# Chunk 0 of an RWKV scan read two tokens a partition, with rstd on ScalarE and a new instruction order

## The chip, the core and the metric

The kernel runs on one core of a Trainium2 chip. A core has five engines, each with its own instruction queue: TensorE (PE, matmuls), VectorE (DVE), ScalarE (ACT), GpSimd (POOL) and SyncE (SP, which here only issues DMAs). Sixteen DMA engines move the data. The metric is the device time of one execution in microseconds, as the median over runs; lower is better.

## What is computed

Two layers in one launch: a linear-attention scan over 768 tokens (4 batches, 8 heads, head size 48), then a LayerNorm and a two-matrix MLP (384 to 1536 to 384) with a residual.

```python
for t in range(S):
    kt, vt, rt = k[:, :, t], v[:, :, t], r[:, :, t]
    cur = np.einsum('bhd,bhe->bhde', u[None] * kt, vt)
    y[:, :, t] = np.einsum('bhd,bhde->bhe', rt, state + cur)
    state = w[None, :, :, None] * state + np.einsum('bhd,bhe->bhde', kt, vt)

x = y.transpose(0, 2, 1, 3).reshape(B, S, H * D)
xn = (x - mean(x)) / np.sqrt(var(x) + 1e-06) * g_ln
out = x + np.maximum(xn @ w_ch1, 0.0) @ w_ch2
```

## The kernel before

The scan is cut into 6 chunks of 128 tokens for each of 4 batches: 24 pieces, numbered `i = 4 * chunk + batch`. Within a piece the decay is folded into the operands: r is multiplied by w^t and k by w^(-1-t), so that the sum over earlier tokens becomes a masked product of two 128-token matrices, and the state `Z` carries what lies before the chunk. Pieces 0 to 3 (chunk 0) have no state behind them.

One piece passes through these steps, whose two- or three-letter names are functions of the kernel and stand in the order table:

- `LR`, `LK`, `LV` (lines 329, 326, 332) issue the loads of r, k, v from SP. A token lies on a partition, and each of its 8 heads is 48 numbers, 192 bytes, at another place in memory.
- `SR`, `SK` scale r and k by the tables `Fr` and `Fk` into the bf16 tile `sc`; `CV` casts v into `vv`. All three go through helpers at lines 194 and 191.
- `TR` (line 348) transposes both on PE; `TCr`, `TCk` or `TC` copy the result from PSUM to `trs`. `Q` (194) multiplies r and k for the `u` term.
- `AT` (371) makes the 8 products of 128 by 128, `AM`, `AMa`, `AMb` (381) mask them into `A`.
- `S` (402, 409, 415) makes the `u` term and the new state, `CC`, `ZU`, `ZD` take them out of PSUM, and `VB` (434) scales v by the `u` term.
- `Y` (444, 452) makes the output, `X` (459) adds `VB` and sums the row, `SQ` (466) squares, `XN` (472, 474) centres.
- `LT` (512) and `XT` transpose the centred rows on PE, or `LT2`, `LTD` do so by DMA.

The MLP follows in 17 groups of one or two pieces (`GROUPS`): `UP` (527) is the first product, `RL` (543, 545) the ReLU, `RS` (480, 483) makes 1/std on POOL in two instructions, `DN` (557) is the second product, `OT` (615) adds the residual and `STO` (622) stores. `LW1` loads a third of `w_ch1` (line 301), and `SW` (308, 310, 312) scales a third of a third into bf16; `LW2` (318) and `CW` do the same for `w_ch2`, into the same fp32 tiles.

The first part of the launch makes the tables: `WF`, `LC` load w, u and the gain; `WB` (269) spreads w over the partitions on PE; `TL` loads the activation table; `LN`, `FK`, `FR` make the logarithm, `Fk` and `Fr` on ACT; `CT`, `CP` turn w, u and the gain into columns; `DU` (261, 265) are matmuls of zeros whose result nobody reads.

Nothing is scheduled by the compiler: `PLAN` is a text of steps `name,piece,engine`, and each engine runs its own instructions in the order in which the text names them. `SLOTS` gives the number of buffers of each ring.

```python
    for step in PLAN.split():
        name, i, e = step.split(",")
        steps[name](int(i), e)
```

## Time and profile before

| | |
|---|---|
| median of 3 runs | 149.1 us (147.78 to 149.59) |
| profiled execution, its own time | 148.24 us |
| its span, first to last instruction | 146.5 us |
| PE, DVE, POOL, ACT busy | 93%, 75%, 64%, 55% of the span |
| mean granted TensorE clock | 0.965 |
| packets moved by DMA | 99267, of which 94508 under 512 B |

Busy shares are means over stages that differ, so the stage has to be looked at by itself. A row of the windows gives, for a stretch of time, each engine's busy microseconds with its number of instructions in brackets, then the granted TensorE clock as a share of full speed, the mean busy share of the 16 DMA engines, and the GB/s that they moved. In the timelines a row is start, duration, engine, line, operation, `out<-in`, shapes and a count of merged instructions; in square brackets stands idle time before it and what ended it. In the chain of waits a row is start, duration, engine, tile and line of the work that ended last at that time. Instructions of one engine overlap at their ends, so two that follow each other take less than the sum of their durations.

### The profile page before, as it was taken

How to read it: one execution, taken by the hardware profiler on the slowest of the kernel's cores; microseconds unless marked ns; L12 is line 12 of the kernel's file. 1: busy time of each engine (PE TensorE's matmuls, PEld its weight loads, DVE VectorE, ACT ScalarE, POOL GpSimd, SP SyncE). 2: the span in 40 equal slices, each digit the busy share in tenths (PEclk: the TensorE clock that was granted, in tenths of full speed). 3: DMA queues.
4: the chain of work that ended last, by engine and by line, in shares of the span. 5: the costliest groups of instructions: out<-in, count | busy, mean ns of one | idle time of the engine just before them, and what ended most of it. 6: DMA issues, size and time to landing. Idle time of an engine off the chain costs nothing.

```text
span 146.5 us, 4250 instructions
## 1 busy us (share of the span) xinstructions
PE 135.8 (93%) x1693; PEld 108.2 (74%) x1693; DVE 110.5 (75%) x220; ACT 80.1 (55%) x175; POOL 94.0 (64%) x132
## 2 busy tenths in 40 slices
PE   3966699999999999999999999999999999999991
PEld 1455477998687897787688887966877777888871
DVE  4569999767969899985959948897946796875232
ACT  2575577977676467466386560663654752244600
POOL 4089878967888999989957493428553076644030
PEclk9999556999999999999999999999999999999999
DMA  5999899999889999899999999988999997830114
GB/s 97 209 211 221 175 277 401 194 258 380 231 170 188 206 197 232 156 215 242 96 229 206 260 233 186 217 166 185 245 157 199 229 184 156 206 123 0 54 37 182
DMA packets 99267, 28.59 MB, mean 195 GB/s; under 512 B 94508, under 2 KB 97712, under 8 KB 99248
## 3 DMA queue, kind: packets, MB, share of 16 engines
q1 hardware_dynamic: 98352, 27.24, 86.3%
q10 hardware_dynamic: 896, 1.09, 2.0%
q8 instruction: 13, 0.21, 0.6%
q14 instruction: 6, 0.05, 0.1%
HBM read 18.88 MB, written 4.72 MB: 161 GB/s over the span
## 4 chain that ended last, share of the span: by engine, by line
PE 60%; SPq 11%; DMA 11%; DVE 7%; POOL 6%; issue 4%; DVEq 0%; POOLq 0%
PE hp L527 17%; PE o L557 16%; PE s L557 7%; PE s L527 5%; SPq L332 4%; DMA w_f<-in_moe_w_ch_dram 4%; SPq L329 4%; SPq L326 3%; DMA trs<-sc 3%; DMA rf<-in_r_dram 3%; PE o L527 3%; PE at L371 2%; PE hp L452 2%; POOL sc L194 2%; PE at L348 2%
## 5 line engine op out<-in xcount | busy, mean ns | idle before, releaser
L527 PEld LDWEIGHTS <-w_sb 128*128 128x128 bf16 x612 | 47.9, 114 | 2.4 <-POOL w_sb L312 0.4
L527 PE MATMUL hp<-xT,w_sb 128*128 128x128 bf16 (+1 forms) x408 | 39.9, 244 | 0.3 <-POOL w_sb L312 0.3
L557 PEld LDWEIGHTS <-hT 128*128 128x128 bf16 x276 | 25.2, 97 | 13.7 <-issue 0.4
L557 PE MATMUL o<-w_sb,hT 128*128 128x384 bf16 x180 | 34.5, 326 | 0.0
L543 ACT ACTIVATE hT<-hp 128x512 bf16<-128x512 f32 x41 | 24.3, 597 | 18.2 <-PE hp L527 17.7
L381 DVE TENSOR_TENSOR A<-at,mask 128x1024 bf16<-128x1024 f32 (+1 forms) x27 | 28.9, 1096 | 1.2 <-PE at L371 1.2
L194 POOL TENSOR_TENSOR sc<-kf,Fk 128x384 bf16<-128x384 f32 x14 | 14.5, 1044 | 10.5 <-DMA kf<-in_k_dram 10.4
L434 POOL TENSOR_TENSOR Vb<-vf,cc 128x384 f32<-128x384 f32 x17 | 14.7, 868 | 8.7 <-ACT cc L189 3.6
L557 PE MATMUL s<-w_sb,hT 128*128 128x384 bf16 x96 | 18.9, 326 | 0.2 <-DVE x L459 0.2
L194 POOL TENSOR_TENSOR q<-trs 128x512 bf16<-128x512 bf16 x11 | 13.4, 1220 | 5.5 <-PE hp L527 2.6
L194 POOL TENSOR_TENSOR sc<-rf,Fr 128x384 bf16<-128x384 f32 x12 | 13.0, 1082 | 5.3 <-DMA rf<-in_r_dram 5.3
L466 ACT ACTIVATE sqj<-x,sm 128x384 bf16<-128x384 f32 x24 | 14.7, 611 | 1.4 <-DVE x L459 1.3
L615 DVE SCALAR_TENSOR_TENSOR ot<-o,rs,x 128x384 f32<-128x384 f32 x15 | 9.2, 613 | 4.5 <-POOL rs L483 2.8
L459 DVE SCALAR_TENSOR_TENSOR x<-hp,Vb 128x384 f32<-128x384 f32 x19 | 10.5, 554 | 2.3 <-PE hp L452 1.6
L483 POOL TENSOR_TENSOR rs<-rs,expo 128x1 f32<-128x1 f32 (+1 forms) x17 | 10.6, 625 | 1.4
L472 ACT ACTIVATE xn<-x,sm 128x384 bf16<-128x384 f32 x13 | 8.0, 613 | 5.7 <-DVE x L459 5.6
L371 PE MATMUL at<-trs 48*128 48x128 bf16 x192 | 8.6, 229 | 2.4 <-ACT trs L189 1.2
L527 PE MATMUL s<-xT,w_sb 128*128 128x128 bf16 (+1 forms) x120 | 10.8, 235 | 0.0
L194 POOL TENSOR_TENSOR Z<-ZS,WLZ 128x384 bf16<-128x384 f32 x10 | 10.3, 1030 | 0.6 <-DVE ZS L428 0.6
L545 DVE TENSOR_SCALAR hT<-hp 128x512 bf16<-128x512 f32 x9 | 6.2, 689 | 4.6 <-PE hp L527 4.6
L371 PEld LDWEIGHTS <-trs 48*128 48x128 bf16 x192 | 6.0, 99 | 4.9 <-ACT trs L189 2.1
L194 DVE TENSOR_TENSOR sc<-rf,Fr 128x384 bf16<-128x384 f32 x12 | 7.5, 633 | 2.3 <-DMA rf<-in_r_dram 2.2
(116 smaller groups left out, 214.3 us busy)
## 6 DMA issues: line engine op xcount, KB each, us to landing
rf<-in_r_dram SPq DMA_DIRECT2D x24, 192.0 KB, 3.8
kf<-in_k_dram SPq DMA_DIRECT2D x24, 192.0 KB, 3.9
vf<-in_v_dram SPq DMA_DIRECT2D x24, 192.0 KB, 3.9
w_f<-in_moe_w_ch_dram SPq DMA_DIRECT2D x6, 768.0 KB, 7.2
out_dram<-ot SPq DMA_DIRECT2D x18, 192.0 KB, 3.4
out_dram<-ot ACTq DMA_DIRECT2D x5, 192.0 KB, 2.0
trs<-sc SPq DMA_TRANSPOSE x12, 3.9
xT<-xn SPq DMA_TRANSPOSE x9, 2.8
```

Of the source, the lines that this page charges most:

```text
L194: engines[e].tensor_tensor(out=out, in0=in0, in1=in1, op=ALU.mult)
L371: nc.tensor.matmul(out=t[:, par, q, :], lhsT=trs(i)[p0 : p0 + D, 1, q, :], rhs=trs(i)[p0 : p0 + D, 0, q, :], start=True, stop=True,)
L381: nc.vector.tensor_tensor(out=AA(i)[:, a:b].rearrange("p e q t -> p (e q) t"), in0=psum["at", i][:, a:b].rearrange("p e q t -> p (e q) t") ...
L434: engines[e].tensor_tensor(out=Vb(i)[:].rearrange("p (h d) -> p h d", h=H), in0=vf(i)[:], in1=cc(i)[:].unsqueeze(2).to_broadcast([P, H, D] ...
L459: nc.vector.scalar_tensor_tensor(out=xx(i)[:], in0=psum["y", i][:, :C], scalar=1.0, in1=Vb(i)[:], op0=ALU.mult, op1=ALU.add, accum_out=sm[ ...
L466: nc.scalar.activation(out=sqj[:], in_=xx(i)[:], func=ACT.Square, bias=sm[i][:], scale=-float(C), accum_out=sq[g][:, j : j + 1])
L472: nc.scalar.activation(out=xn(i), in_=xx(i)[:], func=ACT.Identity, bias=sm[i][:], scale=-float(C))
L483: nc.gpsimd.tensor_tensor(out=rs[g][:], in0=rs[g][:], in1=expo[:, :n], op=ALU.pow)
L527: nc.tensor.matmul(out=t[:, a * gw : (a + 1) * gw].rearrange("p (j t) -> p j t", j=size), lhsT=w1_sb[n][kc][:, fb::FB], rhs=xT(g)[:, :size ...
L543: nc.scalar.activation(out=o, in_=s, func=ACT.Relu)
L557: nc.tensor.matmul(out=psum["o", i][:, :C], lhsT=hT(g)[:, fk, j * P : (j + 1) * P], rhs=w2_sb[d][:, a, :], start=(seen == 0 and a == 0), s ...
L615: nc.vector.scalar_tensor_tensor(out=ot(i), in0=psum["o", i][:, :C], scalar=rs[g][:, j : j + 1], in1=xx(i)[:], op0=ALU.mult, op1=ALU.add,)
```

## The change

For pieces 0 to 3 the layout is another. A tile of `kf`, `rf` or `vf` now holds two pieces. For chunk 0, partition p (0 to 63) holds tokens 2p and 2p+1 of an even batch, and partition 64+p the same tokens of the odd batch: each packet is the 96 numbers of two neighbouring tokens, 384 bytes, and a load is 512 packets instead of 1024. What a step works on as piece `i` is then one token parity of both batches. There are four tables `F0` (k and r, even and odd tokens), made from the powers `pow0`, and masks `mask0` for parities. `AT` makes 16 products with 64 output rows instead of 8 with 128; the state part of `S` takes two pieces of 64 rows, 8 products instead of 4; `Y` of one batch gathers from both parity pieces, 32 products instead of 8. The stores of these pieces write 3072 contiguous bytes from 64 partitions.

`RS` moves to ACT, as `Ln` and `Exp` of a column. `VB` may run on ACT, as 8 instructions of 48 columns. `ln_all` and `Fr` share a tile. The rings `kf`, `rf` go from 11 to 10 buffers, `x` from 14 to 12, `A` from 3 to 4. The whole `PLAN` is in another order with other engines; two of its lines stand for it.

```diff
-SLOTS = {'kf': 11, 'rf': 11, 'vf': 11, ..., 'A': 3, ..., 'x': 14, ...}
+SLOTS = {'kf': 10, 'rf': 10, 'vf': 11, ..., 'A': 4, ..., 'x': 12, ...}
 PLAN = """
-LR,1,- LK,0,- MI,0,g MW,0,v WF,0,s WB,0,- LC,0,s LC,1,s MM,0,g MP,0,v TL,0,s LC,2,s DU,21,h LN,0,s FK,0,s FR,0,s SK,0,v LK,1,- LR,0,- SK,1,v CT,0,o
+MZ,0,g MI,0,g MM,0,g WF,0,s MW,0,v LC,0,s LC,2,s LC,1,s WB,0,h LK,1,- LV,0,- LR,1,- LR,0,- TL,0,s LN,0,s MP,0,v MQ,0,v LK,0,- GK,0,s SK,0,g CT,0,o
...
+    def GK(x, e):
+        nc.scalar.activation(out=F0[x][1][:], in_=ln_all[:], func=ACT.Exp, scale=pow0[:, x, 1:2])
+    def GR(x, e):
+        nc.scalar.activation(out=F0[x][0][:], in_=ln_all[:], func=ACT.Exp, scale=pow0[:, x, 0:1])
...
+    def load(ring, pair, src, i):
+        if i >= B:
+            nc.sync.dma_start(out=ring(i), in_=chunk_src(src, i))
+        else:
+            b0 = i % 2 * DP
+            nc.sync.dma_start(
+                out=pair[i // 2][b0 : b0 + DP].rearrange("p a h d -> p (a h d)").rearrange("p (h x) -> p h x", h=H),
+                in_=src[i, :, :L, :].rearrange("h (p j) d -> p h (j d)", j=2),
+            )
...
     def SK(i, e):
-        times(e, sck(i)[:, :, :D], kf(i)[:], Fk[:])
+        times(e, sck(i)[:, :, :D], rows_of(kf, kp, i), Fk[:] if i >= B else F0[i % 2][1][:])
...
     def AT(i, e):
         t = psum["at", i] = ps_a.tile([P, 2, HP, P], FP32, name="at")
+        if i < B:
+            for q in range(HP):
+                for b0 in (0, DP):
+                    for par in range(2):
+                        p0 = par * DP
+                        nc.tensor.matmul(
+                            out=t[b0 : b0 + DP, par, q, :].rearrange("p (j t) -> p j t", j=2),
+                            lhsT=trs(i)[p0 : p0 + D, 1, q, b0 : b0 + DP],
+                            rhs=tp[i // 2][p0 : p0 + D, :, 0, q, b0 : b0 + DP],
+                            start=True,
+                            stop=True,
+                        )
+            return
...
     def VB(i, e):
+        if e == "s":
+            for h in range(H):
+                nc.scalar.activation(out=o[:, h], in_=rows_of(vf, vp, i)[:, h], func=ACT.Copy, scale=cc(i)[:, h : h + 1])
...
     def Y(i, e):
+        if i < B:
+            x = i % 2 * DP
+            for a in (i - i % 2, i - i % 2 + 1):
+                for par in range(2):
+                    for q in range(HP):
+                        h = 2 * q + par
+                        for b0 in (0, DP):
+                            nc.tensor.matmul(
+                                out=t[b0 : b0 + DP, h * D : (h + 1) * D], lhsT=AA(a)[b0 : b0 + DP, par, q, x : x + DP],
+                                rhs=vv(a)[b0 : b0 + DP, h, :],
+                                start=first, stop=True, skip_group_check=True,
+                            )
+                        first = False
+            return
...
     def RS(g, e):
-        nc.gpsimd.tensor_scalar(
-            out=rs[g][:], in0=sq[g][:], scalar1=1.0 / C, scalar2=1e-6 * C * C, op0=ALU.mult, op1=ALU.add
-        )
-        nc.gpsimd.tensor_tensor(out=rs[g][:], in0=rs[g][:], in1=expo[:, :n], op=ALU.pow)
+        nc.scalar.activation(out=rs[g][:], in_=sq[g][:], func=ACT.Ln, bias=eps[:], scale=1.0 / C)
+        nc.scalar.activation(out=rs[g][:], in_=rs[g][:], func=ACT.Exp, scale=-0.5)
```

At three places the order counts most. The rows below give the line, the operation, the tile written (its number is that of a buffer) and the tiles read.

ACT at the start of the program, before: the table load stands ahead of the last small DMA, and two tables follow the logarithm.

```order
L204 DMA w_row<-in_w_dram 1x384
L212 DMA rows<-in_w_dram 4x2x48
L212 DMA rows<-in_u_dram 4x2x48
L230 ACT_TABLE_LOAD
L210 DMA rows<-in_moe_g_ln_dram 3x128
L272 ACTIVATE ln_all<-s 128x384
L277 ACTIVATE Fk<-ln_all,pow_i 128x384
L280 ACTIVATE Fr<-ln_all,pow_i 128x384
L189 COPY trs_112<-hp 128x512 x2
L189 COPY cols<-o 128x11
```

And ACT at the same place now, where the tile `Fr` first holds the logarithm:

```order
L220 DMA rows<-in_moe_g_ln_dram 3x128
L222 DMA rows<-in_u_dram 4x2x48
L240 ACT_TABLE_LOAD
L307 ACTIVATE Fr<-hp 128x384
L273 ACTIVATE F_01_214<-Fr,pow_217 128x384
L199 COPY cols<-o 128x11
L312 ACTIVATE Fk<-Fr,pow_i 128x384
L276 ACTIVATE F_10_215<-Fr,pow_217 128x384
L276 ACTIVATE F_00_213<-Fr,pow_217 128x384
L273 ACTIVATE F_11_216<-Fr,pow_217 128x384
L315 ACTIVATE Fr<-Fr,pow_i 128x384
L199 CAST vv_91<-vf_79 128x384
```

All four small DMAs now stand ahead of the table load, and six tables are made where two were, with the copy of the columns and a cast of v among them.

SP around the first load of `w_ch1`, before (`w_f` is its fp32 tile; 18 loads of r, k, v stand ahead of it, of which these are the last):

```order
L329 DMA rf_85<-in_r_dram 128x8x48
L332 DMA vf_94<-in_v_dram 128x8x48
L332 DMA vf_95<-in_v_dram 128x8x48
L332 DMA vf_96<-in_v_dram 128x8x48
L301 DMA w_f_243<-in_moe_w_ch_dram 128x3x512
```

And SP there now, where 17 loads stand ahead of it, 12 of them with the new 64x8x96 shape:

```order
L368 DMA vf_80<-in_v_dram 64x8x96
L365 DMA rf_76<-in_r_dram 128x8x48
L368 DMA vf_80<-in_v_dram 64x8x96
L365 DMA vf_81<-in_v_dram 128x8x48
L365 DMA rf_76<-in_r_dram 128x8x48
L365 DMA kf_71<-in_k_dram 128x8x48 x2
L336 DMA w_f_228<-in_moe_w_ch_dram 128x3x512
```

The load of v for piece 5 has moved behind the three loads of `w_ch1`; the other 17 are still ahead of them.

ACT before the first `UP` product, before (`w_sb` is the scaled part of `w_ch1`, `xT` the transposed rows, `hT` what `RL` writes):

```order
L189 COPY xT_157<-o 128x384
L189 CAST vv_110<-vf_94 128x384
L189 COPY cc_126<-o 128x8
L466 ACTIVATE sqj,sq_192<-x_141,sm_168 128x384
L189 COPY trs_112<-at 128x1024
L189 COPY xT_158<-at 128x384
L472 ACTIVATE xn_155<-x_142,sm_169 128x384
L189 COPY cc_127<-hp 128x8
L308 ACTIVATE w_sb_1_247<-w_f_243,g_neg 128x512
```

And now:

```order
L507 ACTIVATE Vb_118<-vf_79,cc_105 128x48 x8
L558 ACTIVATE xn_134<-x_123,sm_148 128x384
L199 COPY trs_97<-hp 128x1024
L199 CAST vv_94<-vf_81 128x384
L552 ACTIVATE sqj,sq_172<-x_123,sm_148 128x384
L343 ACTIVATE w_sb_1_232<-w_f_228,g_neg 128x512
L343 ACTIVATE w_sb_0_231<-w_f_228,g_neg 128x512
L199 COPY xT_137<-at 128x384
L199 COPY xT_138<-at 128x384
```

Both transposed rows are now copied after the weights are scaled, and the eight-part `VB` stands ahead of them all.

On PE, the first `UP` now comes ahead of the two products `AT` of pieces 4 and 5, of `S` of piece 5, of `Y` of piece 4 and of the `LT` of piece 2, all of which stood before it.

More of the change, by code (lines that the diff above doesn't have):

```diff
@@ L356, in TC @@
     def TC(i, e):
-        copy(e, trs(i)[:], psum["tr", i][:].rearrange("p (a q) t -> p a q t", a=2))
+        copy(e, trs(i), psum["tr", i][:].rearrange("p (a q) t -> p a q t", a=2))
     def Q(i, e):
@@ L412, in S_ @@
                 )
-            flat = sck(i).rearrange("p (q e) d -> p q (e d)", e=2)
-            for q in range(HP):
-                nc.tensor.matmul(
-                    out=t[:, q * E2 : (q + 1) * E2], lhsT=flat[:, q, :], rhs=vv(i)[:, 2 * q : 2 * q + 2, :],
-                    start=False, stop=True, skip_group_check=True,
-                )
+            if i >= B:
+                parts = [(i, slice(0, P))]
+            else:
+                b0 = i % 2 * DP
+                parts = [(i - i % 2 + x, slice(b0, b0 + DP)) for x in range(2)]
+            for a, rows_ in parts:
+                flat = sck(a).rearrange("p (q e) d -> p q (e d)", e=2)
+                for q in range(HP):
+                    nc.tensor.matmul(
+                        out=t[:, q * E2 : (q + 1) * E2], lhsT=flat[rows_, q, :], rhs=vv(a)[rows_, 2 * q : 2 * q + 2, :],
+                        start=False, stop=True, skip_group_check=True,
+                    )
     def CC(i, e):
@@ L497, in TKR @@
         nc.sync.dma_start_transpose(
[L498 removed]
+            out=trs(i).rearrange("p a q t -> p (a q) t"), in_=sc(i)[:].rearrange("p a h d -> p (a h d)")
         )
```

162 lines of the change are left out of this document (99 added, 63 removed).

## The prediction

> **What bounds the kernel now.** I read first the page's rows of slices, then the windows of the first 25 us, then the chain of waits, then the timelines of the engines in that part. From the page:
>
> ```profile
> PE   3966699999999999999999999999999999999991
> PEclk9999556999999999999999999999999999999999
> ```
>
> A slice is 3.66 us. From the seventh on, PE is full and its clock is whole. So the kernel has two parts: a start of some 25 us in which PE is not full, and 118 us in which PE's work sets the time. A change pays if PE becomes full earlier, less what work it then still has ahead.
>
> ```profile
> 5.00:10.00 5.00, 4.29 (x42) 2.79 (x41) 3.41 (x8) 2.75 (x8) 2.44 (x4) 1.00 1.08 216
> 10.00:15.00 5.00, 2.75 (x57) 2.28 (x56) 4.93 (x12) 3.22 (x9) 4.58 (x5) 0.90 1.07 210
> 15.00:20.00 5.00, 3.96 (x42) 2.97 (x43) 5.00 (x12) 2.47 (x8) 3.97 (x5) 0.50 0.89 179
> 20.00:25.00 5.00, 4.83 (x75) 3.92 (x72) 4.88 (x12) 3.94 (x10) 4.34 (x6) 0.58 1.02 381
> ```
>
> In these windows DVE (third pair) is full from 10 to 25, the DMA engines are full too, at 213 GB/s (mean of 216 and 210) while r, k, v come in 192-byte packets and at 381 while w_ch1 comes in 2048-byte ones, and PE's clock is halved from about 14.6 to 25. In the chain of waits the end of this part and a later place:
>
> ```profile
> 17.72 5.84 DMA w_f<-in_moe_w_ch_dram
> 23.67 1.38 POOL w_sb L312 x2
> 25.10 0.86 PE hp L527 x12
> ...
> 28.81 0.17 PE hp L444 x4
> 28.98 0.20 PE hp L452 x8
> ...
> 37.08 0.55 PE at L371 x16
> 37.63 0.76 PE s L557 x4
> ...
> 39.06 0.65 PE o L557 x4
> ```
>
> The first UP starts at 25.10, released by the scaling of w_ch1, which waited for its load. So three things end near 25 us: the load, DVE, and PE at half clock.
>
> **The loads.** A load is 196,608 bytes: at 213 GB/s 0.92 us. A packet takes each of 16 engines 16 x 192 B / 213 GB/s = 14.4 ns, one of 2048 B at 381 GB/s 86.0 ns. On the line between them one of 384 B takes 14.4 + 192 x (71.6 / 1856) = 21.8 ns, so a load of 512 packets, 32 an engine, takes 0.70 us. The ends are 0.92 (the rate stays) and 196,608 / 381 = 0.52 us (it is already full). I take 0.70, since the two rows differ by a fixed part and a part by bytes. The Trainium skill speaks against more: DMA: Bandwidth & Descriptors, section Why small descriptors are slow, has a fixed 3 cycles a packet beside its 32-byte beats, and the section How a descriptor splits into AXI transactions lets beats count from a 256-byte boundary; by both, 12 cycles for 192 B and 17 for 384 B, an estimate of 0.65 us a load. No row here shows a packet of 384 B.
>
> ```profile
> DMA to landing us min/median/max: 2.9/3.8/4.4
> 0.72 0.46 SPq L329 DMA_DIRECT2D rf<-in_r_dram  x1
> ```
>
> The first load of r was issued at 0.72 and landed 2.9 later (the row is over ten loads), at 3.6; with 0.92 of transfer it began at about 2.0 and needed 0.7 to be seen. So load n lands at 2.0 + n x 0.70 + 0.7. The tenth (last r of pieces 2, 3): 9.7, against 11.9 at the old rate. The first third of w_ch1 (786,432 B, 2.06 us at 381) stands behind 12 new loads and 5 old ones: 2.0 + 8.4 + 4.6 + 2.06 + 0.7 = 17.8. Before it landed at 23.56. The load ceases to be what ends last.
>
> **The walk through the start.** Rows for what follows:
>
> ```profile
> 3.84 2.31 PE L261 MATMUL hp<-warm 128*128 128x512 bf16 x5
> 7.32 1.06 PE L348 MATMUL hp<-ident,sc 128*128 128x128 bf16 x16
> ...
> 5.31 1.03 DVE L194 TENSOR_TENSOR sc<-kf,Fk 128x384 bf16<-128x384 f32 x2 [3.00 <-ACT Fk L277]
> 9.07 0.65 DVE L194 TENSOR_TENSOR q<-trs 128x512 bf16<-128x512 bf16 x1 [0.23 <-ACT trs L189]
> 9.98 3.07 DVE L381 TENSOR_TENSOR A<-at,mask 128x512 bf16<-128x512 f32 x5
> 13.63 0.55 DVE L194 TENSOR_TENSOR Z<-hp,WLZ 128x384 bf16<-128x384 f32 x1
> 14.10 0.55 DVE L459 SCALAR_TENSOR_TENSOR x<-hp,Vb 128x384 f32<-128x384 f32 x1
> 17.25 1.21 DVE L381 TENSOR_TENSOR A<-at,mask 128x1024 bf16<-128x1024 f32 x1
> ...
> 2.78 1.28 ACT L230 ACT_TABLE_LOAD   x1 [2.78 <-DVE expo L255]
> 2.82 0.42 ACTq L210 DMA_DIRECT2D rows<-in_moe_g_ln_dram  x1
> 4.67 0.61 ACT L277 ACTIVATE Fk<-ln_all,pow_i 128x384 f32<-128x384 f32 x1
> 7.96 1.07 ACT L189 COPY trs<-hp 128x512 bf16<-128x512 bf16 x2 [2.18 <-PE hp L348]
> 11.34 0.91 ACT L189 CAST vv<-vf 128x384 bf16<-128x384 f32 x2
> 16.75 0.62 ACT L472 ACTIVATE xn<-x,sm 128x384 bf16<-128x384 f32 x1 [0.29 <-DVE x L459]
> 19.72 0.62 ACT L466 ACTIVATE sqj<-x,sm 128x384 bf16<-128x384 f32 x1
> 20.68 1.01 ACT L189 COPY trs<-at 128x1024 bf16<-128x1024 bf16 x1 [0.25 <-PE at L348]
> 21.59 0.48 ACT L189 COPY xT<-at 128x384 bf16<-128x384 bf16 x1
> 23.65 0.72 ACT L308 ACTIVATE w_sb<-w_f,g_neg 128x512 bf16<-128x512 f32 x1 [0.78 <-DMA w_f<-in_moe_w_ch_dram]
> ...
> 7.49 1.00 POOL L194 TENSOR_TENSOR sc<-rf,Fr 128x384 bf16<-128x384 f32 x1 [5.28 <-DMA rf<-in_r_dram]
> 10.20 1.15 POOL L194 TENSOR_TENSOR q<-trs 128x512 bf16<-128x512 bf16 x1
> ```
>
> The first two transposes come later. The table load stands behind a fourth DMA issue of 0.42 us, so the logarithm ends near 5.0 instead of 4.6. The four F0 tables and Fk take 0.55 each, with the copy of the columns among them: the even table of r ends at 7.3, the odd one of k at 7.9. The product of r follows on DVE to 7.9. But 39 quarter units of empty matmuls (9 of 512 columns, 3 of 128) now stand ahead of the transposes and behind the product of the columns, which waits for three small DMAs until about 4.9. At the 0.46 us of the row for five they would end at 9.3; the 66 ns of a transpose in the next row shows the faster clock at 7.3, so I take 8.5. Transposes to 9.4, 11 more units to 10.0, copies of trs on ACT, two of 0.53 behind a cast, to 10.1, the first AT at 10.2, the first mask at 10.75, 0.8 later than the 9.98 before.
>
> From there DVE's order sets the pace: two masks (0.61 each) to 12.0; Z waits for S, which stands behind the transposes of piece 3 on PE, for which POOL scales r after 9.7: 10.7, S by 11.7; so Z to 12.5, a mask, Q (0.4) and a mask to 14.05, a copy (0.35), the product of r (0.5) and Z to 15.4, the mask of piece 3 (1.2, after 0.25 of waiting for Y and AT) to 16.85, the first X at 17.35, Z and the second X to 18.3. On ACT, XN of that first X ends at 17.95, then the full copy of trs (18.9), a cast (19.4), SQ (20.05, w_ch1 long there), two scalings (21.35) and xT (21.8). POOL, with Q and two products of about 1.0 behind the loads of piece 4 and 5, then XN and its scaling, is done by 20.8. So the first UP starts at 21.8 instead of 25.1: 3.3 us earlier.
>
> **What is moved behind it.** PE has still to do: two AT (the 0.55 row of L371), Y of a piece (0.17 and 0.20, L444 and L452), S (four products of L444's width and about as much for the u term and the state: 0.35), LT (three transposes, 0.18): 1.45 us. This comes off.
>
> **More products on PE.** AT has 8 more for each piece, S 4, Y 24. By the row of L452 a small product takes 25 ns; from above, its weight load by itself is some 0.1 us. So 36 x 4 = 144 products cost 3.6 us, at worst 14, all ahead of the first UP, where PE had 2.25 us idle of 5 between 10 and 15 alone. I take 25 ns and no cost on the path beyond the walk, where Y counted 0.9; a rival takes the other end. The switch to half-height also costs: the L557 group behind AT takes 0.76 instead of 0.65. Here that is some 20 switches, 2 us, in the same cover. TensorEngine Tiling (Array Packing) in the Trainium skill, section Key Properties, says that a change of tiling mode drains the engine; that row agrees, and gives it 0.11 us.
>
> **RS and VB.**
>
> ```profile
> L483 POOL TENSOR_TENSOR rs<-rs,expo 128x1 f32<-128x1 f32 x10 | 5.6, 559 | 0.8
> L480 POOL TENSOR_SCALAR rs<-sq 128x1 f32<-128x1 f32 x10 | 2.1, 211 | 5.8 <-ACT sqj L466 5.2
> L466 ACT ACTIVATION_READ_ACCUMULATOR sqj<-x,sm 128x1 f32 x24 | 4.6, 190 | 0.0
> ```
>
> RS takes 0.77 us from POOL 17 times, 13 us, and puts two columns of 0.19 us on ACT, 6.5 us. ACT is 55% busy, so that lies beside PE's work; behind RS on ACT wait RL and xT, late by 0.4 us at most. Bounds: nothing, or 17 x 0.4 = 7 us if PE waited each time; RL alternates with DVE, so I take 0. VB on ACT is eight parts of about 0.2 us, 1.6 against 0.83 on POOL; only piece 0's lies in the start, and ACT waits there for X anyway. The tail has the same work; a half store is now issued by ACT, 0.3 us of issue beside the last DVE part: 0.15.
>
> **Sum.** -3.3 + 1.45 + 0.15 = -1.7 us. Against the profiled execution, 148.24 (span 146.5, 1.7 around it), that is 146.5; it lies 0.9 below the median of the runs shown, so for the median 149.1 I forecast 147.4.
>
> **Rivals.**
>
> The half clock binds (slower). PE's rows show the clock halved after a window in which it was 2.75 of 5 busy, and still halved at 3.96. In the walk it waits for DVE and POOL between 10 and 17 too. If the clock halves near 14 again, the products from the first Y (14.1) on, some 6.7 us at full clock, take 13.4, and UP begins at 27.5; if the clock returns after 3 us of it that are spared, at 24.5. The time is 147.4 + 2.7 to 5.7, so 150.1 to 153.1. It decides from UP at 23.5 on, where the gain of 1.7 is used up. For it: 144 more products that each occupy PE. Against: PE is busier than before there, and the empty matmuls. TensorE: Matmul & The Clock Gate in the Trainium skill, Part 1, has the clock follow PE's activity over windows of 3.4 us; the trace agrees, with the faster clock seen at 7.32, 3.5 us after the empty matmuls began at 3.84.
>
> The 384-byte packet moves no faster, which is the change not doing what it says: r of piece 3 lands at 11.9 instead of 9.7, S and everything behind it on DVE 2.0 later, UP at 23.8: 149.4. DMA: Bandwidth & Descriptors in the Trainium skill, first table, asks 512 B for line rate, which would allow this; that the rows at 192 and 2048 B differ by a part for bytes speaks against.
>
> The earlier start is lost again in the new order, since other waits stand in 118 us of PE's work (RS behind RL, DMA transposes late): 149.1. For it: nearly every engine's order changed. Against: PE was kept full before by an order of the same kind, with the DMAs now ahead.
>
> More is gained: small tables and masks are quicker, UP at 20.3 and a later microsecond of idle PE closed: 147.4 - 2.5 = 144.9.
>
> **The numbers.** The forecast 0.45, the half clock 0.2, no faster packet 0.08, lost in the order 0.12, more gained 0.15. Two per cent is 3.0 us (about what a measurement of this kernel can tell from no change): 146.1 and 152.1. Faster takes the last rival and a quarter of the forecast's own spread (1.5 us): 0.15 + 0.11, so 0.26. Slower takes the upper third of the first rival and some of the lost order: 0.07 + 0.04, so 0.11. Same: 0.63. The range 144.7 to 151.0 holds 0.8: it reaches to the last rival and into the half clock, and leaves 0.07 out below and 0.13 above.
>
> **What would show it.** Loads of chunk 0: the windows from 2 to 10 us at about 280 GB/s, w_f landed by 18. First L610 (UP) on PE near 21.8, with ACT's xT as its releaser, and the chain of waits in the start on DVE and ACT, not on SP. The clock: no 5 in its row at slices 4 to 6, or the first rival. PE's row full from slice 6 on; idle of PE after 25 us over 2 us would speak for the order. DVE waiting for ACT at OT would show RS. If UP starts by 22 and the time is not lower, my split into a start and a full part is wrong.

## The result and the profile after

The changed kernel takes 153.14 us in the median of four executions (152.77 to 154.48), the kernel before beside it 148.9 (147.78 to 149.59). It is slower by 4.2 us, 1.028 times as long by these medians. The ratio on record, which counts only the faster of two states in which executions of a kernel fall, is 1.036, with a 95% interval of 1.030 to 1.043; for the runs below, this ratio to the kernel before as it ran beside them stands in brackets with its interval. I had forecast 147.4 in a range up to 151.0; the time lies just above the upper end of the first rival (half clock, 150.1 to 153.1), which I had given a chance of 0.2. Its profiled execution took 153.01 us, with a span of 151.2 against 146.5.

The rows of slices of the changed kernel, a slice 3.78 us (before 3.66):

```profile
PE   3398959999999999998999979999999999999992
PEclk9999995699999999999999999999999999999999
```

PE now idles in the second slice (3, before 9) and in the sixth (5, before 9), and the half clock has not gone: its 5 and 6 stand in slices 7 and 8 instead of 5 to 7. The windows of the start (columns as before: PE, PE's weight loads, DVE, ACT, POOL, clock, DMA share, GB/s):

```profile
2.00:4.00 2.00, 1.55 (x2) 0.49 (x2) 0.33 (x3) 0.75 (x1) 1.74 (x11) 1.00 0.56 139
4.00:6.00 2.00, 0.06 (x1) 0.00 (x0) 0.34 (x2) 1.64 (x3) 0.01 (x1) 1.00 1.09 253
6.00:8.00 2.00, 1.62 (x5) 0.93 (x6) 0.00 (x0) 1.01 (x3) 0.00 (x0) 1.00 1.27 218
8.00:10.00 2.00, 2.00 (x6) 0.76 (x5) 1.80 (x3) 1.79 (x4) 1.12 (x1) 1.00 1.30 222
...
20.00:22.00 2.00, 0.62 (x8) 0.45 (x8) 2.00 (x7) 0.95 (x2) 2.00 (x2) 1.00 1.03 378
22.00:24.00 2.00, 1.88 (x22) 1.72 (x23) 1.97 (x7) 2.00 (x5) 2.00 (x4) 0.60 1.05 405
24.00:26.00 2.00, 2.00 (x51) 1.56 (x48) 1.43 (x2) 1.11 (x3) 2.00 (x3) 0.50 1.12 348
```

The loads of chunk 0 run at 218 to 253 GB/s, not 280, and at 139 in the first window, where only 0.56 of the DMA engines' time is used. DVE does nothing from 6 to 8 us. From 20 to 22 PE works 0.62 of 2 us, and from 22 on its clock is halved. The timelines say what each engine waited for in that start (PE, DVE, ACT, POOL in turn):

```profile
6.38 0.57 PE L229 MATMUL o<-idr,rows 11*128 11x11 f32 x2 [2.32 <-DMA rows<-in_u_dram]
6.88 4.02 PE L296 MATMUL hp<-warm 128*128 128x512 bf16 x9
11.01 1.06 PE L399 MATMUL at<-ident,sc 128*128 128x128 bf16 x8
21.00 0.62 PE L399 MATMUL hp<-ident,sc 128*128 128x128 bf16 x8 [1.18 <-POOL sc L204]
...
8.20 1.06 DVE L204 TENSOR_TENSOR sc<-rf,F 128x384 bf16<-128x384 f32 x2 [3.79 <-ACT F L276]
9.21 2.37 DVE L204 TENSOR_TENSOR sc<-kf,F 128x384 bf16<-128x384 f32 x3
12.66 0.42 DVE L201 COPY trs<-o 128x512 bf16<-128x512 bf16 x1 [0.80 <-PE o L399]
14.27 1.27 DVE L445 TENSOR_TENSOR A<-at,mask 128x512 bf16<-128x512 f32 x2
20.11 0.54 DVE L545 SCALAR_TENSOR_TENSOR x<-hp,Vb 128x384 f32<-128x384 f32 x1
...
6.99 0.17 ACT L199 COPY cols<-o 128x11 f32<-128x11 f32 x1 [1.30 <-PE o L229]
...
8.88 1.24 POOL L204 TENSOR_TENSOR sc<-kf,F 128x384 bf16<-128x384 f32 x1 [4.87 <-DMA kf<-in_k_dram]
13.06 1.00 POOL L204 TENSOR_TENSOR sc<-rf,F 128x384 bf16<-128x384 f32 x1 [1.88 <-DMA rf<-in_r_dram]
```

The columns' product waited for its small DMA until 6.38, not 4.9; ACT stood 1.30 us behind it with three of the four tables still to make; the empty matmuls ran at 0.45 us each to the end, so the transposes came at 11.01; POOL, which waited for the loads, began on k of piece 0 at 8.88 and on r of piece 3 at 13.06. DVE stood 0.80 us for the transposes before it could copy them at 12.66. The first mask starts at 14.27 instead of 9.98. The chain of waits shows the end of the start:

```profile
14.08 4.84 DMA kf<-in_k_dram
19.95 1.00 POOL sc L204
20.95 1.13 POOL q L204
...
25.78 0.98 PE hp L528 x17
27.62 2.16 PE hp L610 x24
```

The first `UP` (L610) begins at 27.42, against 25.10 before, 2.3 us of the 4.7 by which the span is longer. The rest lies behind it: 123.8 us from there to the end, against 121.4.

### The profile page after: what moved, and what is told of

Read it like the earlier page. It is cut to its first block, busy times and chain, and to the rows that moved or that the text cites. A ratio compares the mean times of both kernels' runs of the same rounds, so it can differ in the third digit from the quotient of the medians.

```text
span 151.2 us, 4597 instructions
## 1 busy us (share of the span) xinstructions
PE 139.2 (92%) x1843; PEld 112.2 (74%) x1843; DVE 113.4 (75%) x224; ACT 86.4 (57%) x228; POOL 88.2 (58%) x115
## 4 chain that ended last, share of the span: by engine, by line
PE 65%; DMA 10%; SPq 10%; DVE 7%; issue 3%; POOL 2%; ACT 2%; DVEq 0%; ACTq 0%
PE hp L610 19%; PE o L640 12%; PE s L640 11%; DMA vf<-in_v_dram 7%; SPq L368 6%; PE o L610 4%; DMA kf<-in_k_dram 3%; PE at L435 3%; DVE A L445 3%; PE s L610 3%; SPq L365 2%; PE at L399 1%; PE hp L485 1%; PE hp L538 1%; PE hp L516 1%
## 5 line engine op out<-in xcount | busy, mean ns | idle before, releaser
L610 PEld LDWEIGHTS <-w_sb 128*128 128x128 bf16 x612 | 49.8, 115 | 3.1 <-issue 0.6
L610 PE MATMUL hp<-xT,w_sb 128*128 128x128 bf16 (+1 forms) x456 | 42.0, 242 | 0.4 <-DVE x L545 0.4
L445 DVE TENSOR_TENSOR A<-at,mask 128x1024 bf16<-128x1024 f32 (+1 forms) x27 | 29.2, 1097 | 3.3 <-PE at L435 3.3
L640 PE MATMUL o<-w_sb,hT 128*128 128x384 bf16 x144 | 27.4, 326 | 1.2 <-ACT hT L626 1.0
L640 PE MATMUL s<-w_sb,hT 128*128 128x384 bf16 x132 | 25.4, 326 | 0.0
L204 POOL TENSOR_TENSOR Vb<-vf,cc 128x384 f32<-128x384 f32 x14 | 11.9, 852 | 9.0 <-issue 4.2
L204 POOL TENSOR_TENSOR sc<-kf,Fk 128x384 bf16<-128x384 f32 x14 | 14.6, 1048 | 2.7 <-DMA kf<-in_k_dram 2.1
L199 ACT CAST vv<-vf 128x384 bf16<-128x384 f32 x11 | 5.5, 508 | 11.0 <-DMA vf<-in_v_dram 11.0
L560 POOL TENSOR_SCALAR xn<-x,sm 128x384 bf16<-128x384 f32 x12 | 7.3, 611 | 7.5 <-DVE x L545 7.3
L201 POOL CAST vv<-vf 128x384 bf16<-128x384 f32 x10 | 6.0, 603 | 5.3 <-DMA vf<-in_v_dram 4.8
L610 PE MATMUL o<-xT,w_sb 128*128 128x256 bf16 (+1 forms) x84 | 9.1, 250 | 0.0
L399 PEld LDWEIGHTS <-sc 128*128 128x128 bf16 x96 | 6.7, 108 | 2.1 <-POOL sc L204 1.8
L698 DVE SCALAR_TENSOR_TENSOR ot<-s,rs,x 128x384 f32<-128x384 f32 x11 | 6.7, 611 | 1.5 <-PE s L640 1.5
```

The source lines that it names most:

```text
L204: engines[e].tensor_tensor(out=out, in0=in0, in1=in1, op=ALU.mult)
L399: nc.tensor.transpose(out=t[:, a * HP + q, :], in_=flat[:, q, :], identity=ident[:])
L445: nc.vector.tensor_tensor(out=AA(i)[:, a:b].rearrange("p e q t -> p (e q) t"), in0=psum["at", i][:, a:b].rearrange("p e q t -> p (e q) t") ...
L560: engines[e].tensor_scalar(out=xn(i), in0=xx(i)[:], scalar1=-float(C), scalar2=sm[i][:], op0=ALU.mult, op1=ALU.add)
L610: nc.tensor.matmul(out=t[:, a * gw : (a + 1) * gw].rearrange("p (j t) -> p j t", j=size), lhsT=w1_sb[n][kc][:, fb::FB], rhs=xT(g)[:, :size ...
L640: nc.tensor.matmul(out=psum["o", i][:, :C], lhsT=hT(g)[:, fk, j * P : (j + 1) * P], rhs=w2_sb[d][:, a, :], start=(seen == 0 and a == 0), s ...
```

## Experiments: how fast the loads are

The runs are called e1 to e17 in the order in which they were made. e1 to e4 look at the size of the packet, with one time each, beside 147.91 for the kernel before. In e1 and e2 the kernel before keeps its 128 partitions and its order, and chunk 0 holds other values of r, k and v; in e3 and e4 those of the kernel after are other ones.

```diff
# e1, before: 4 packets of 96 numbers a partition (e2: 2 of 192)
-        nc.sync.dma_start(out=kf(i)[:], in_=chunk_src(k, i))
+                in_=src[i, :4, : 2 * L, :].rearrange("h (p j) d -> p h (j d)", j=2),
```

> The kernel before, in which each load of chunk 0 takes 384-byte packets onto all 128 partitions (4 heads of 256 tokens instead of 8 heads of 128, so the values of chunk 0 are others; bytes and everything else stay). Theory A (a packet under 512 B costs by its bytes, so 384 B moves no faster): the DMA row of the windows from 3 to 12 us stays at 205 to 235 GB/s and w_ch1 lands within 0.5 us of the 23.6 of before. Theory B (the half-height shape, 64 partitions, is what held the loads of the changed kernel back): 270 GB/s or more, w_ch1 lands by 21.5.

> As the run before, with 768-byte packets on 128 partitions (2 heads of 512 tokens; the values of chunk 0 are others). Theory A (a step near 512 B): over 330 GB/s, unlike at 384 B. Theory B (a smooth fixed part for each packet): about 330 GB/s too, with 384 B at 280. Together with the 384-byte run it separates a step from a slope. If UP waits only for w_ch1 in the kernel before, it starts by 22.5 instead of 25.1; if DVE or PE's half clock hold it as well, it stays after 24.

Measured: 147.13 and 146.7. The windows of e1, 4 to 10 us:

```profile
4.00:6.00 2.00, 2.00 (x6) 0.59 (x4) 0.72 (x2) 1.65 (x4) 0.00 (x0) 1.00 1.04 264
6.00:8.00 2.00, 2.00 (x15) 1.65 (x14) 1.38 (x3) 0.00 (x0) 0.90 (x1) 1.00 1.10 297
8.00:10.00 2.00, 1.69 (x20) 1.38 (x17) 0.76 (x3) 1.55 (x5) 1.69 (x3) 1.00 1.14 278
```

A mean of 280 GB/s: the line between two packet sizes was right at 384 B, for 128 partitions. It doesn't hold at 768 B: the same windows of e2 show 261, 263 and 305, no more than with 384 and below what both theories expected. And loads a third faster moved the first `UP` of the kernel before only from 25.10 to 24.83 (24.95 with 768 B). That doesn't make the loads free. In e1 `w_ch1` landed near 20.9 instead of 23.56, but PE worked from 19.89 to 24.83 without a pause, at half its clock up to 24:

```profile
20.00:22.00 2.00, 2.00 (x27) 1.71 (x27) 1.97 (x5) 1.40 (x4) 2.00 (x3) 0.50 1.05 408
```

So when the load no longer ends last, PE at half clock does, 0.3 us ahead of it.

```diff
# e3, after: 192 bytes a packet on the same 64 partitions (e4: 768)
-                in_=src[i, :, :L, :].rearrange("h (p j) d -> p h (j d)", j=2),
+                in_=src[i].rearrange("h t d -> (h t d)")[...].rearrange("(p m z x) -> p m z x", m=16, z=2, x=48)[:, :, 0],
```

> The changed kernel with packets of 192 B on 64 partitions in chunk 0 (1024 packets a load, wrong rows, same bytes). Theory A (bytes decide): loads land as in the changed kernel, the tenth near 13.0 us, time 152.5 to 154. Theory B (the 64-partition shape costs by packets, so the larger packet did help): the tenth lands after 15 us and the time is over 154.5.

> The changed kernel with packets of 768 B on 64 partitions in chunk 0 (256 packets a load, wrong rows, same bytes). If packet size limits the loads: over 330 GB/s, the tenth load lands before 9.5 us. If 64 partitions limit them: below 250 GB/s, the tenth still after 12 us. If late loads are what made the changed kernel slow, the time falls by 2 us or more; if the order of its tables and empty matmuls did, by less than 1.

Measured: e3 153.53 with 192 B (180 GB/s from 6 to 12 us, where the kernel before moves 213 in the same packets), e4 151.82 with 768 B (219 to 258). At each size 64 partitions are slower than 128. These two and the kernel after have one order and differ in their packets alone, and here faster loads do move the start: with 192, 384 and 768 B POOL begins on r of piece 3 at 14.28, 13.06 and 12.56, and the first `UP` is at 29.10, 27.42 and 26.24.

e5 is the kernel after with another order of its first loads. Odd and even pieces lie in different halves of the partitions; the kernel after alternates in its first four loads too, and the largest move is k of piece 0 from the fifth place to the second:

```diff
-MZ,0,g ... LK,1,- LV,0,- LR,1,- LR,0,- ... LK,0,- ...
+MZ,0,g ... LK,1,- LK,0,- LR,1,- LR,0,- LV,1,- LV,0,- LK,3,- LK,2,- LR,3,- LR,2,- LV,3,- LV,2,- ...
```

> The changed kernel with its 12 loads of chunk 0 issued so that neighbours go to different halves of the partitions (k of batches 1, 0, then r, then v, then 3, 2), nothing else moved. Theory A (a load on 64 partitions reaches half of the DMA engines' paths, and only the mix of the two halves in flight matters): 3 to 12 us at over 250 GB/s, k of piece 0 lands by 6.5 instead of 8.8 us, time down by 1 us or more. Theory B (a 64-partition load is slow by itself, in any mix): 210 to 235 GB/s as before, k of piece 0 earlier only by its place in the queue, time within 1 us of 153.1.

Measured: e5 151.78 (1.022, 1.013 to 1.031), 1.4 us below the kernel after by the medians, 0.7 by what each has over the kernel before that ran beside it. With loads to the two halves of the partitions in turn, 4 to 10 us show 255, 245 and 241 GB/s (253, 218 and 222 in the kernel after). The first mask comes at 13.40; that isn't shown to be the loads' doing, since e10 below, the same up to there, has it at 14.46, with slower empty matmuls and transposes (4.02 us for the nine large empties against 3.76, 1.06 for eight transposes against 0.61). The first `UP` is still at 27.02: PE stood idle for 1.60 us up to 20.56, and its clock was halved from there on.

## Experiments: RS, and the order of the tables

```diff
# e6: the columns behind the empty matmuls
-... CT,0,o CP,0,s FK,0,s UW,0,g GR,1,s SR,1,v DU,39,h GR,0,s ... FR,0,s LK,2,-
+... FK,0,s GR,1,s SR,1,v DU,39,h CT,0,p GR,0,s ... FR,0,s CP,0,s UW,0,g LK,2,-
```

> The changed kernel with the product of the columns behind the empty matmuls on PE, and their copy behind all tables on ACT. Theory A (late loads of chunk 0 and 1 set the first UP): the tables end 1.3 us earlier and the first transpose starts by 10.3 instead of 11.0, but UP starts within 0.6 us of 27.4 and the time stays within 1 us of 153.1. Theory B (the serial start of tables and empty matmuls sets it): UP by 26, time 151.8 or less.

e7 is the kernel before with the `RS` of the kernel after (the plus lines of `RS` in the diff of the change), e8 the kernel after with that of the kernel before (its minus lines).

> The kernel before with 1/std on ScalarE (logarithm and exponential of a column) in the places of its order where GpSimd had it. If RS is part of the loss: 1 us or more slower than before, with VectorE waiting for ScalarE at the residual. If it is free, as I forecast: within 0.7 us of before.

> The changed kernel with 1/std back on GpSimd, in the same places of the order. If RS on ScalarE costs the changed kernel: 1 us or more below 153.1. If not, 152.5 to 154.5, or slower, since its order gave GpSimd other work.

Measured: e6 153.58 (1.036, 1.028 to 1.045): transposes at 8.91, two us earlier, but the first mask only at 13.25, since DVE then waited 1.17 us for k, the clock halved from 15 on and the first `UP` at 28.11. Taking away one early wait made the start worse. e7 149.76 (1.010, 1.002 to 1.018), 1.5 us above the kernel before, within two per cent of it; e8 157.9 (1.066, 1.058 to 1.075). A wait of DVE in the kernel before and what stands in its place in e7, then PE's waits of e7 and of e8 (total, number, longest):

```profile
DVE ot L615 <- POOL rs L483: 2.8, 4, 1.0
...
DVE ot L612 <- ACT rs L480: 5.4, 6, 1.5
...
PE o L524 <- DVE ot L612: 0.7, 1, 0.7
PE hp L452 <- DVE A L381: 0.6, 2, 0.5
...
PE o L643 <- POOL w_sb L201: 1.5, 2, 1.3
PE hp L516 <- ACT hT L629: 0.7, 1, 0.7
```

`RS` is not free on ACT in the old order: DVE waits for ACT at `OT`, the sign that I had named, 5.4 us in all where it had waited 2.8 for POOL, and PE then waits for DVE. On POOL it is far worse in the new order, which has put other work on POOL, and in the kernel after no wait of DVE for `rs` is listed. Each order fits its own place for `RS`; the move by itself costs 1.5 us in the old order (0.3 to 2.7 by the interval of e7). What it costs in the new one no run shows.

## Experiments: the half clock, empty matmuls, product height

```diff
# e9, before: empty matmuls in the gaps of the start
-... TR,1,h TCk,1,v ... AT,1,- LV,1,- ... Y,0,h X,0,v ... Y,1,- X,1,v ... DU,3,p
+... TR,1,h DU,12,p TCk,1,v ... AT,1,- DU,16,p LV,1,- ... Y,0,h DU,16,p X,0,v ... Y,1,- DU,8,h X,1,v ... DU,12,p
# e10, on e5; e15, on the kernel after
-... Y,0,h X,0,v ... TR,4,h TC,4,s
+... Y,0,h DU,24,o X,0,v ... TR,4,h DU,8,o TC,4,s
# e11, on the kernel after
-DU,39,h
+DU,1,h
```

> The kernel before, with 61 more quarter units of empty matmuls in the gaps of its start (behind the transposes of piece 1, behind AT and Y of piece 0, behind Y of piece 1, ahead of the transposes of piece 4), nothing else changed. Theory (the start is bound by the half clock from 14 to 24 us): no 5 in the clock's row before 25 us, the first UP by 23.5 instead of 25.1, the time 1.5 us lower or more (146.7). Rival (DVE and POOL bind the start and the clock only follows): the clock stays up, but the first UP stays within 0.4 of 25 and the time within 0.5 of the kernel before. Third: the empty matmuls themselves stand ahead of work and UP goes to 26 or later.

> The kernel after with the loads of chunk 0 alternating between the halves of the partitions (as in the earlier run, 151.8), and 32 more quarter units of empty matmuls behind Y of piece 0 and the transposes of piece 4, where PE stood still for 1.6 us before its clock halved. Theory (the late start costs PE its clock, and the half clock from 21 to 29 us makes the rest of the loss): clock 1.0 from 14 on, the first UP by 25 instead of 27.0, the time at or below 150.3. Rival (waits of DVE and POOL set the first UP): UP at 26.5 or later, time 151.3 or more.

> The kernel after with one quarter unit of empty matmuls ahead of the first transposes instead of 39. Theory (the empties ran at the low clock from 6.9 to 10.9 us but are not what is late: k of piece 0 and the tables are): the first transposes at 9.5 to 10.2 instead of 11.0, cold; the first mask gains less than 0.5 (from 14.3 to 13.8 or later) since products then run at the low clock; the first UP within 1 of 27.4; the time within 1 of 153.1. Rival (the empties are the late step): first mask by 12.8, UP by 25.5, the time 1.5 lower or more.

Measured: e9 149.5 (1.006, 1.000 to 1.013). The clock is 1.00 in every window, and the first `UP` comes at 25.01, 0.09 earlier, behind the scaling of `w_ch1`, which waited for its load:

```profile
25.01 0.86 PE L527 MATMUL hp<-xT,w_sb 128*128 128x128 bf16 x12 [0.59 <-POOL w_sb L312]
...
23.59 1.37 POOL L312 TENSOR_SCALAR w_sb<-w_f,g_neg 128x512 bf16<-128x512 f32 x2 [0.65 <-DMA w_f<-in_moe_w_ch_dram]
```

So in the kernel before two things end together near 25. e1 takes away the load, and PE at half clock holds `UP`; e9 takes away the half clock, and the load holds it. Neither gains over 0.3 us alone, and no run takes away both. DVE, which in both kernels is busy for 14.91 us between 10 us and `UP` (of 15.1 and 15.0), comes close behind: in e9 the last product ahead of `UP`, which needs one of its masks, ends at 24.42, so by an estimate from that row the two together would have gained some 0.7 us while DVE's work stays where it is.

e10 151.1 (1.019, 1.006 to 1.033), clock 1.0 throughout, `UP` at 26.03 instead of 27.02: between my two theories. e11: the executions spread from 149.97 to 154.19, so only the start in the profile of one of them (153.35) is read: transposes at 9.14 instead of 11.01, first mask at 13.12 instead of 14.27, clock halved from 15.8 us on, `UP` at 27.51. The empty matmuls delay the mask by 1.15 us in it, more than the 0.5 that I expected, and without them `UP` comes no earlier; the clock is halved there, but that this alone takes the gain back isn't shown (the mean clock of the execution of 149.97 was 0.997, that of the one of 154.19 was 1.000).

e12 is e10 with products of full height (chunk 0 gets other values):

```diff
# AT and Y
-        if i < B:
+        if False:
# S
-        if i >= B:
+        if True:
```

> The kernel of the last run with alternate loads and empty matmuls (151.1, first UP 26.0), in which AT, S and Y of chunk 0 are made in products of full height (8, 4 and 8 instead of 16, 8 and 32), so that chunk 0 has other values; loads, tables and order unchanged. Theory (the first UP follows DVE, which works without a pause from the first mask on; PE's more and smaller products lie in its idle time): first UP within 0.4 of 26.0, time within 0.5 of 151.1. Rival (the half-height products and the switches of height lie on the path): first UP by 25.0, time 150.2 or less.

Measured: e12 150.24 (1.013, 1.006 to 1.021), first `UP` at 25.74, 0.3 earlier. The time is 0.9 below e10's, more than I expected, though the intervals overlap; by what each has over the kernel before beside it (148.42 and 148.96) it is 0.3. So the 144 extra products cost between nothing and 0.9 us, and which isn't settled: e12's clock, unlike e10's, was 0.50 from 18 to 20 us and 0.69 from 20 to 22.

> The kernel after itself, loads and order as they are, with 32 quarter units of empty matmuls behind Y of piece 0 and the transposes of piece 4. If the half clock of 22 to 29 us makes part of its loss, as the rival of the prediction has it: clock 1.0 from 14 to 30, first UP by 26.6 instead of 27.4, time lower by 0.7 or more (152.4). If it makes none: UP within 0.4 of 27.4 and the time within 0.4 of 153.1. If it makes the whole loss: UP by 24, time 150 or less.

Measured: e15 151.9 (1.015, 1.006 to 1.025), 1.2 us below the kernel after by the medians, 2.8 by what each has over the kernel before beside it (150.44 here); the span of the profiled execution is 1.1 shorter. Its windows, beside those of the kernel after above, its first `UP`, and POOL's scaling of k of piece 4:

```profile
20.00:22.00 2.00, 1.75 (x15) 0.85 (x13) 2.00 (x7) 0.61 (x1) 2.00 (x3) 1.00 1.03 384
22.00:24.00 2.00, 1.94 (x36) 1.33 (x35) 1.70 (x5) 1.98 (x5) 2.00 (x3) 1.00 1.05 408
24.00:26.00 2.00, 2.00 (x78) 1.64 (x73) 1.97 (x5) 2.00 (x6) 2.00 (x4) 1.00 1.07 366
...
25.94 0.94 PE L610 MATMUL hp<-xT,w_sb 128*128 128x128 bf16 x14
...
19.34 1.00 POOL L204 TENSOR_TENSOR sc<-kf,Fk 128x384 bf16<-128x384 f32 x1 [1.29 <-DMA kf<-in_k_dram]
```

With the gap at 20 us filled, the clock stays whole and the first `UP` comes at 25.94 instead of 27.42. TensorE: Matmul & The Clock Gate in the Trainium skill, Part 1, has the clock follow PE's activity; these two runs agree, since nothing but empty products was added. The rest of the lateness is there at full clock too. The chain of waits of e15 reaches `UP` as that of the kernel after does, through the load of k of piece 4 and POOL's products behind it: 6.60 us from the start of its scaling to `UP`, against 8.43 in the kernel after (18.99 to 27.42).

## Experiments: an earlier start

```diff
# e13, on e10: all four tables ahead of the columns and of Fk
-... CT,0,o CP,0,s FK,0,s UW,0,g GR,1,s SR,1,v DU,39,h ... TR,1,o FR,0,s SK,3,v SK,2,v ... AT,0,- AMa,0,v AMb,0,v
+... GR,1,s SR,1,v DU,39,h CT,0,p ... TR,1,o CP,0,s UW,0,g FK,0,s FR,0,s SK,3,v SK,2,v ...
# e14, on e13: and DVE's two scalings behind the masks
+... DU,30,h CT,0,p ... FR,0,s ... AT,0,- AMa,0,v SK,3,v AMb,0,v SK,2,v
# e16, on e14: empty matmuls in the gap behind AT of piece 0, fewer later
+... AT,0,- DU,24,p AMa,0,v ... Y,0,h DU,8,o X,0,v ... TR,4,h DU,4,o
# e17, on e16: S of piece 0 ahead of the transposes of piece 3 (DU,24 is split into 16 and 8)
+... S,0,o CC,0,s ZU,0,v SK,2,v DU,8,p TR,3,h AT,1,-
```

> The kernel with alternate loads and empty matmuls, with the columns' product, its copy and the table Fk put behind the four tables of chunk 0, so that ACT makes these without the wait of 1.5 us for the columns. Theory (the start is bound by DVE, whose first scaling begins at 8.2 instead of 5.3 because of the tables): first scaling on DVE by 6.6, the first UP 0.8 or more earlier than 26.0, the time 150.4 or less. Rival (the loads of r and k, or the empty matmuls ahead of the transposes, hold the start as much): DVE begins earlier but waits, the first mask stays within 0.7 of 14.5 or the first UP within 0.4 of 26.0.

> As the last, with 30 instead of 39 quarter units of empty matmuls ahead of the first transposes, and with DVE's two scalings of k of pieces 3 and 2 put behind the first masks instead of ahead of the copies of the transposes. Theory: with tables, loads and DVE's order put right, the start gains what I had forecast: first mask by 11.8, first UP by 24.3 with the clock at 1.0, time 149.3 or less. Rival (w_ch1, landed at 26 to 27, or k of piece 4 is the next bound): first mask by 11.8, but first UP at 25 or later or a wait of PE for w_sb of 1 us or more, time 150 or more. What is left over 147.4 then lies behind the first UP: waits of PE after 28 us of 1.5 or more would show the order's part.

Measured: e13 154.47 and e14 154.0, both with executions far apart (149.76 to 155.47, and 152.8 to 165.91; e14's ratio is 1.035, 1.025 to 1.045), so that only the start in their profiles (154.57 and 165.91) is read. In e13 DVE begins at 7.28 instead of 8.39 in e10, waits 1.76 us for k of piece 2 or 3, and the first mask comes at 12.78; in e14 at 12.07. PE stands still in both: in e13 for 1.72 us until DVE has copied the transposes, and for 0.68 until POOL has scaled r of piece 3, in e14 for 1.64 until POOL has scaled r. The clock is halved from 13 and from 15 us on, and the first `UP` comes at 29.47 and 28.82, where the kernel after has 27.42. In these two executions an earlier first mask with a wait behind it was a loss; the one of e13 that took 149.76 kept a clock of 1.00, so the loss isn't in every one.

> The kernel with tables first and DVE's masks first (the last run of the call before, 154.0), with 24 quarter units of empty matmuls in the gap behind AT of piece 0, where PE stood still for 1.64 us ahead of r of piece 3 and lost its clock, and 12 instead of 32 later on. If that gap is what turned the earlier start into a loss: clock 1.0 from 10 to 24 us, first UP by 26.0, time 151.2 or less. If r of piece 3 (landed at about 12.3) is the bound behind the masks, no more than that is gained: transposes of piece 3 still at 13.4 to 13.7, UP not below 25.2. Rival (DVE's early start carries through): UP by 24.3, time 149.5 or less.

> As the last, with S of piece 0, its copy and its Z moved ahead of the transposes of piece 3, so that DVE's Z of piece 0 doesn't wait for r of piece 3. If this wait was the bound: Z of piece 0 on DVE by 14.2 instead of 15.2, first UP 0.8 or more earlier than in the last run. If DVE's own work is (16 us of it ahead of the first UP, begun at 7.3): UP moves by less than 0.4. Neither would be faster than the kernel before: from a first UP at 24.5, with 1.45 moved behind it, I expect 149.5.

Measured: e16 151.4 (1.013, 1.006 to 1.021), e17 152.05 (1.015, 1.003 to 1.026). In e16 the clock stays at 1.00. DVE's first mask, PE's transposes of piece 3, the POOL products that they and the next piece waited for, and the first `UP`:

```profile
11.32 0.69 DVE L436 TENSOR_TENSOR A<-at,mask 128x512 bf16<-128x512 f32 x1
...
13.57 0.62 PE L390 MATMUL hp<-ident,sc 128*128 128x128 bf16 x8 [0.90 <-POOL sc L195]
25.22 1.50 PE L601 MATMUL hp<-xT,w_sb 128*128 128x128 bf16 x24
...
12.52 2.26 POOL L195 TENSOR_TENSOR sc<-rf,F 128x384 bf16<-128x384 f32 x2 [3.79 <-DMA rf<-in_r_dram]
18.63 1.00 POOL L195 TENSOR_TENSOR sc<-kf,Fk 128x384 bf16<-128x384 f32 x1 [0.87 <-DMA kf<-in_k_dram]
```

The first mask is at 11.32, near my 10.75, and yet `UP` starts at 25.22: r of piece 3 (12.5) and k of piece 4 (18.6) land too late. From that k to `UP` it is 6.59 us, as in e15. The span is 149.3, 2.8 us over the kernel before's, though `UP` starts only 0.1 later than there: that 2.7 lies behind it. In e17 DVE's Z of piece 0 ran at 12.80 instead of 14.95, and the first `UP` came at 25.66, no earlier. DVE then waited for PE and for r of a later piece instead (0.66 and 0.74 us). None of the kernels with the reference's values was faster than the kernel before.

## Why the prediction was wrong, step by step

The sum had -3.3 for an earlier first `UP`, +1.45 for work moved behind it, +0.15 for the tail: -1.7. The span came out at +4.7, 6.4 more. Of these, 5.6 lie ahead of the first `UP` (27.42 instead of 21.8). The first, third and fourth of these points add up to that; the second is a cause that stands behind them:

- **The first mask, 3.5 us late (14.27 instead of 10.75).** This step failed most, and on PE's side of it. The columns' product came at 6.38 instead of 4.9, 1.5 late. The 39 quarter units behind it ended at 11.0, 4.6 us later, not 3.6: I let the clock rise among them, but the nine large ones took 4.02 us, 0.45 each to the last. From the transposes to the mask it took 3.26 instead of 2.25: the first eight transposes took 1.06 us, and `Q` on DVE 1.03 beside POOL's scaling. DVE's three scalings of k, which I had walked through as if they were done, and the late loads were not on this path: DVE was done with them at 11.9 and waited for the transposes. They come onto it as soon as the transposes are earlier (DVE waits 1.17 us for k in e6, 1.76 in e13). So the steps aren't additive: e6 and e11, which take away one each, gained 1.0 and 1.15 at the mask and nothing at `UP`. e16, with tables, empties and DVE's order changed together and the loads in turn, has the mask at 11.32.
- **The loads, and a second way to `UP` that the walk didn't follow.** The load of 0.70 us was interpolated from rows of 128 partitions, and the new loads have 64: at 218 to 253 GB/s it is 0.78 to 0.90, after a first window at 139. By my formula k of piece 4, the sixteenth load, lands at 14.8; POOL began on it at 18.99. From there to `UP` it takes 6.6 us at full clock (e15, e16), so `UP` at 21.8 needed it by 15.2, whatever the first mask did. That shows in e16: its mask is 2.8 us ahead of e15's, its `UP` 0.7. I had written that the chain of waits would be on DVE and ACT and not on SP; in the kernel after and in e15 it runs through SP's issues, this load and POOL. Which of SP's issuing (0.6 to 0.9 us for most of these loads) and the transfers sets the pace isn't shown.
- **From mask to `UP` at full clock, 0.75 us more.** 11.05 in the walk, 11.8 in e15 (14.14 to 25.94). That this is close says little for the walk, in which DVE's order sets the pace: with an earlier mask the stretch grows, to 13.9 in e16, since the loads hold its end.
- **The half clock, 1.35 us.** Mask to `UP` took 13.15 in the kernel after, 1.35 more than in e15. This is my first rival in its price, not in its cause: it had the clock halve near 14 with PE's longer work, and here it is halved from 22.4 to 29.2, after PE idled 1.18 us ahead of the transposes of piece 4. That the time came out at the end of that rival's range is partly luck, since the late loads and mask make up the most of it.

Behind the first `UP` the term of 1.6 measures 2.4 (123.8 against 121.4). It belongs to the new order, at half clock or not: 123.8 to 124.5 us from `UP` to the end in the kernel after, e5, e10, e15 and e16, 120.5 to 122.6 in the kernel before, e1 and e9. For the 1.45 of moved work alone no run was made, nor for the 0.15 of the tail. PE's waits behind 28 us add up to 1.8 us against 1.0 in the kernel before, 1.0 of them one wait for `hT` from ACT near 89 us; 1.45, 0.15 and these 0.8 more would be the 2.4, and the 0.8 belong to the rival "lost in the new order". That sum fits, but no run shows it, and the clock is still halved for 1.8 us behind `UP` in the kernel after.

By point: **loads**, wrong (0.70 holds for 128 partitions, e1). **Clock**, I had it as a rival, and read it right as one of the things that end near 25 in the kernel before: taking it away alone gained nothing there (e9), since the load ends with it. (It is halved from 14.0 to 24.2 there, not from 14.6 to 25.) **Half-height products**, from 0 to 0.9 us (e12), so near the 0 that I took, not the 3.6 to 14 of the bound. **RS on ACT**, not nothing: some 1.5 us in the old order (e7), while the new one needs it (e8). **VB on ACT**, eight parts in 1.91 us instead of 1.6. **The premise** was short: that the loads were what to make earlier. In the kernel before, loads at 280 GB/s gained 0.27 us at `UP` (e1), for PE at half clock ended 0.3 us ahead of them and DVE's work some 0.7; I had seen that three things end near 25 and credited an earlier load with 3.3 us.

What makes the 4.2 us up, then: the half clock 1.2 by the medians (e15; 2.8 by the kernels before beside them) and the loads in turn 0.7 to 1.4 (e5). They overlap, since both together give 2.0 (e10, 151.1). The 2.1 that remain in e10 are about its 0.9 of later `UP` and the moved work behind it. These two are not shown by a run that undoes them alone; they are how I read it.

## What to carry to other kernels

Where several things end together, an experiment that takes one of them away shows only what it is worth alone: e1 and e9 each moved `UP` by less than 0.3 us, and what each took away held `UP` in the other. Before a stretch is called earlier, find what releases its first instruction, and check that each later input keeps up. A load's rate is measured on the shape that it will have, partitions included, not only on the size of its packets. An earlier start with a wait behind it can gain nothing, and PE's clock can fall in that wait; filling the gap with empty products is a cheap test.

## What the hardware showed that I had not expected

- Loads onto 64 partitions, in the kernels of the new order, are slower than onto 128 in those of the old one at equal packets: 180 against 213 GB/s at 192 B, 218 to 253 against 264 to 297 at 384 B. In the first window of the kernel after the DMA engines were busy for 0.56 of the time and moved 139 GB/s, and e5's order didn't change that (0.60, 137); from 4 us on, loads to the two halves in turn give 241 to 255.
- Idle time of PE of 1.2 to 1.7 us was followed by a halved clock within 2.5 us (kernel after, e5, e13), which then stayed for 6 us or more although PE was busy for 1.88 to 2.00 of each 2 us. The length of the gap alone doesn't decide: in e16 PE stood still for 0.90 us at 12.7, with another 0.69 near 20, and the clock stayed at 1.00; in e11 a gap of 0.90 from 13.07 on was followed by the half clock at 15.8.
- A DVE scaling of 128x384 took 0.53 us alone (two in 1.06 from 8.20 on in the kernel after) and 0.94 while POOL scaled too (e16 at 12.99; three in 2.37 from 9.21 on in the kernel after), up to 1.33 in e14 at 12.68.
